# A fused attention and MLP kernel: GELU's steps queued by a clock of GpSimd's queue, output units in pieces of 7, 8 and 9, up pairs in one and in two double steps, and a block's last up pair amid the units in front of it

## The chip, the cores and the metric

The kernel runs on one core of a Trainium2 chip. A core has five engines with a queue each, which take their instructions in program order: TensorE (PE, matrix products; PEld are its weight loads), VectorE (DVE), ScalarE (ACT), GpSimd (POOL) and SyncE (SP, which here only issues DMAs). They meet through semaphores. The metric is the time of one execution in device microseconds (us), as the median of several runs.

## What is computed

The output mixes an attention and an MLP over the same 2048 tokens of width 576:

```python
def _A_ref(x, wqkv, wo):                     # 32 heads of 18
    q, k, v = split(x @ wqkv)
    p = softmax(einsum("bhqd,bhkd->bhqk", q, k) * 18 ** -0.5)
    return einsum("bhqk,bhkd->bhqd", p, v) @ wo

def _B_ref(x, w1, b1, w2, b2):               # 576 -> 4608 -> 576
    y = layernorm(x)
    return gelu(y @ w1 + b1) @ w2 + b2       # the tanh form of GELU

g = sigmoid((x * gate_w).sum(-1))
return g * A + (1 - g) * B
```

All of it is float32. Where a product needs more than TensorE's rounded float32 gives, an operand is split into a high and a low part, and the product is made of three.

## The kernel before

A prologue of some 270 us makes q, k and v, normalizes x, and stores the parts in DRAM. An epilogue of some 75 us divides by the softmax sums, multiplies by `wo` and mixes. Between them lies the main loop, which is what the change is about.

**The loop's steps.** There are 512 steps: 32 units (a pair of heads and half of the queries) of 16 key chunks. Two steps, an even and an odd one, make a double step, in which the program writes, for PE:

- four *rounds* (`next_round`, `s1_round`, L185): two score products for a later unit, whose row maxima DVE takes (L187). The products go to a pool of three PSUM tiles, and a round uses two of them.
- four *score pairs* (`s2`, L226): the scores of this unit, with the maximum subtracted by two extra rows. They go to one PSUM tile `pss` (there is only one), from which ACT takes the exponential (L228). So a score pair can start only when the exponential before it is done.
- one *P·V* (`pv`, L243): sixteen products of the exponentials of the two steps before with v.
- three *fills* (`fill`): pieces of the MLP. Share 0 closes the even step, shares 1 and 2 lie in the odd one.

Before the change both steps have the same form: round, score pair, then P·V (even) or fill 1 (odd), then round, score pair, then fill 0 or fill 2.

**The MLP in the fills.** `mlp` is a generator. The tokens come in four blocks of 512 (`tb`), the 4608 hidden columns in nine groups of four chunks (`g`); that makes 36 groups. A group has two *up pairs* (`h_pair`, L412; 27 double products, `m` = 0 and 1) and four *output units* (`out_pair`, L481; 24 double products, with a drain of PE in the middle). The order is: up pair 0 of group i, the four units of group i-1, up pair 1 of group i. `cuts` says after which products a unit is interrupted, by the share of the fill in which it begins (`piece`). Before, an output unit that begins in fill 0 has three pieces of eight; up pair 1 has four pieces, and up pair 0 (`last`) as many as bring its end to fill 2. Up pair 1 and the next up pair 0 thus take nine fills, three double steps, and a group seven double steps. When the stream is behind its schedule (`late`), up pair 1 has three pieces, and both take two double steps.

**GELU.** When an up pair has ended, DVE and ACT bring its two halves with the bias from PSUM to the tiles `z` (L431, L432; three buffers). Then follow for each half: square (ACT, L452), `plus(GC0)` (two POOL operations), tanh (ACT, L454), and `parts` (four POOL operations, which give `hh` and `hl`, the parts of the hidden activations). `defer(n, fn)` writes a step n *slots* later, a slot being a call of `run_due`, four to a step. Before, these delays are constants: the tanh stands 7 to 9 slots behind the up pair's end whatever POOL has to do in between.

**The weights.** In the first block the raw weights come from DRAM and are split: ACT rounds (L339), POOL subtracts, and both parts are stored for the later blocks, which reload them (`reload`). `bg` holds these splits; one starts when POOL's estimated load (`load`, lowered by 950 per slot) is under a bound.

**The input of the next block.** `load_y` brings the normalized input to the two tiles `Y`. During a block's last up pair it overwrites them chunk by chunk behind the products that read them; the next up pair reads the new chunks.

Of the kernel before, what the change touches and what calls it, by code (L numbers as in the profile page):

```python
# [16 lines left out]
P = 128  # L17
# [7 lines left out]
TB = 512  # L25
# [18 lines left out]
AHEAD = 1  # L44
# [14 lines left out]
def gated_mix_kernel(ctx: ExitStack, tc: tile.TileContext, x, wqkv, wo, w1, b1, w2, b2, gate_w, out):  # L59
# [61 lines left out]

    bg = []
    load = [0.0]

    def run_due():

        slot[0] += 1
        load[0] = max(load[0] - SLOT, 0.0)
# [5 lines left out]
        while k < len(bg):  # L134
            if load[0] < bg[k][2] and slot[0] >= bg[k][0]():
                bg.pop(k)[1]()
                k = 0
            else:
                k += 1

    def pool_op(n, fn, *args, **kw):

        load[0] += n * (1.25 if fn == nc.gpsimd.tensor_scalar else 2.55)
        fn(*args, **kw)  # L144
# [145 lines left out]
    def mlp():  # L290
# [43 lines left out]
        def split(table, key, pool, shape, raw, src, scr, then):  # L334
# [13 lines left out]
            queue = SLOT if raw[0] == 1 else 100 * SLOT  # L348
# [42 lines left out]
        def h_pair(q, last):  # L391
# [16 lines left out]
            ends = cuts(27, (3, 5, 4)[piece[0]] if last else 3 if late and not open_pairs[0] else 4)  # L408
# [17 lines left out]
            open_pairs[0] = 1  # L426

            lag = 0 if m else 2
# [4 lines left out]
            for h in (1, 0):  # L433
                z = zs[h]
                w = zp.tile([P, TB], F32, name="zz", bufs=3)
                hh = hp.tile([P, TB], F32R, name="hh")
                hl = hp.tile([P, TB], F32R, name="hl")
# [7 lines left out]
                def parts(w=w, z=z, hh=hh, hl=hl, h=h, j=2 * m + h):  # L445
# [8 lines left out]
                defer(7 + lag - h, lambda w=w: nc.scalar.activation(w, w, AF.Tanh, scale=GC1))  # L454
                defer(9 + lag - 2 * h, parts)
# [3 lines left out]
        def out_pair(i, t, acc):  # L459
# [5 lines left out]
            ends = cuts(24, (3, 2, 4)[piece[0]])  # L465
# [39 lines left out]
        def outs(i):  # L505
# [4 lines left out]
            for t in range(4):  # L510
                yield from out_pair(i, t, ACC[tb])
# [16 lines left out]
        q = 0  # L528
        for i in range(n + 1):
            for part in range(2):  # L530
                if i < n:
                    tb, g = seq[i]
                    for m in range(AHEAD) if part == 0 else range(AHEAD, G // 2):
                        prep(q + 2)
                        last = i > 0 if part == 0 else m == G // 2 - 1 and i + 1 == n
                        yield from h_pair(q, last)
                        q += 1
                        if g == NG - 1 and m == G // 2 - 1:
# [495 lines left out]
```

## Time and profile before

| | |
|---|---|
| time, median of three runs | 2476.18 us (2474.2 to 2478.33) |
| the profiled execution | 2478.72 us, its span 2476.9 us |
| granted TensorE clock, mean | 0.982 |
| busy: PE, DVE, ACT, POOL | 2367.3, 1665.6, 1363.3, 965.1 us |
| weight loads on PE | 1604.0 us |
| DMA traffic | 330.40 MB, 133 GB/s in the mean |

The span reaches from the first to the last instruction. PE is busy for 96% of it, but its instructions overlap and their ends are modelled, so a busy PE can still be held up: it shows in the distance from the start of one instruction to the start of the next. In rows of a timeline the first number is the start in us from the span's beginning, the second the duration of the merged group, and behind x stands how many instructions are merged; what stands in brackets is idle time of the engine before them, and what ended it.

### The profile page before, as it was taken

The page shows a single profiled execution, that of the slowest core. Times are in us where ns is not written, and L with a number is a line of the kernel's source. Part 1 is how long each engine was busy: PE and PEld are TensorE (multiplying, and loading weights), DVE is VectorE, ACT ScalarE, POOL GpSimd, SP SyncE. Part 2 cuts the span into 40 slices and gives each one's busy share as a digit, 9 for nine tenths or more (in the row PEclk, how much of TensorE's full clock was granted, in tenths as well). Part 3 has the DMA queues.
Part 4 walks back from the last instruction along what each step waited for, and adds up shares of the span by engine and source line. Part 5 has one row for each costly group of instructions (what it writes and reads, how often), then busy time and mean ns, then how long its engine had stood idle before and what let it go on. Part 6 is the DMA issues. An engine that isn't in the chain of part 4 may idle for free.

```text
span 2476.9 us, 50614 instructions
## 1 busy us (share of the span) xinstructions
PE 2367.3 (96%) x20585; PEld 1604.0 (65%) x20585; DVE 1665.6 (67%) x2890; ACT 1363.3 (55%) x1604; POOL 965.1 (39%) x964
## 2 busy tenths in 40 slices
PE   8998999999999999999999999999989999999978
PEld 7876656666665666666666666666656666666538
DVE  4467566667666777776767777777757777777515
ACT  4222466666665566655655665656546556566551
POOL 3001455555553443333444444333343333444310
PEclk9999899999999999999999999999989999999989
DMA  7747645444456423242264333232364332331245
GB/s 231 243 157 222 187 157 149 126 131 138 127 178 175 131 90 112 92 138 97 96 162 144 107 108 111 90 111 96 106 180 126 115 114 101 93 132 46 70 149 200
DMA packets 164506, 330.40 MB, mean 133 GB/s; under 512 B 57826, under 2 KB 84486, under 8 KB 153438
## 3 DMA queue, kind: packets, MB, share of 16 engines
q1 hardware_dynamic: 161970, 322.45, 42.1%
q10 hardware_dynamic: 2304, 4.72, 0.5%
q8 instruction: 162, 2.65, 0.5%
q14 instruction: 70, 0.57, 0.1%
HBM read 234.31 MB, written 96.73 MB: 134 GB/s over the span
## 4 chain that ended last, share of the span: by engine, by line
PE 62%; DMA 4%; issue 3%; ACT 2%; DVE 2%; POOL 1%; SPq 0%; ACTq 0%; POOLq 0%
PE ps L481 15%; PE ps L243 15%; PE ps L412 14%; PE pss L226 9%; PE ps L185 8%; DMA big<-y_scr 2%; PE ps L940 2%; DVE m L187 1%; ACT p L228 1%; ACT z L432 1%; POOL zz L144 1%; ACT ring L228 0%; DMA x<-in_B_w_dram 0%; DMA ka<-ot_scr 0%; POOL w L144 0%
## 5 line engine op out<-in xcount | busy, mean ns | idle before, releaser
L187 DVE TENSOR_REDUCE m<-ps 128x1 f32<-128x512 f32 x2048 | 1315.7, 685 | 548.9 <-PE ps L185 541.8
L228 ACT ACTIVATE p<-pss 128x1024 f32<-128x1024 f32 x684 | 700.2, 1024 | 530.8 <-PE pss L226 530.5
L412 PE MATMUL ps<-big,w 64*128 64x512 f32 x3888 | 539.1, 400 | 23.0 <-ACT z L432 11.5
L481 PE MATMUL ps<-w,hh 64*128 64x288 f32 x4608 | 514.8, 298 | 13.2 <-issue 0.5
L144 POOL TENSOR_SCALAR zz<-zz 128x512 f32<-128x512 f32 x288 | 178.2, 619 | 878.3 <-ACT zz L452 719.8
L226 PE MATMUL pss<-qa,ka 56*128 56x512 f32 x2048 | 466.5, 433 | 42.6 <-ACT p L228 25.9
L185 PE MATMUL ps<-ka,qa 54*128 54x512 f32 x2048 | 478.3, 427 | 13.0 <-DVE m L187 5.6
L228 ACT ACTIVATE ring<-pss 128x1024 f32<-128x1024 f32 x340 | 348.1, 1024 | 257.9 <-PE pss L226 257.8
L412 PEld LDWEIGHTS ps<-big,w 64*128 64x128 f32 x3888 | 400.6, 188 | 109.9 <-ACT z L432 25.2
L481 PEld LDWEIGHTS ps<-w,hh 64*128 64x128 f32 x4608 | 394.4, 185 | 70.0 <-issue 47.2
L144 POOL TENSOR_TENSOR zz<-zz,z 128x512 f32<-128x512 f32 x288 | 370.4, 1286 | 24.0
L185 PEld LDWEIGHTS ps<-ka,qa 54*128 54x128 f32 x2048 | 220.1, 186 | 231.0 <-DVE m L187 195.2
L243 PE MATMUL ps<-p,vt 128*32 128x512 f32 x2736 | 351.0, 608 | 1.4 <-DMA vt<-v_scr 1.4
L481 PE MATMUL ps<-w,hl 64*128 64x288 f32 x2304 | 351.1, 292 | 0.0
L226 PEld LDWEIGHTS pss<-qa,ka 56*128 56x128 f32 x2048 | 209.4, 188 | 147.2 <-ACT p L228 85.2
L144 POOL TENSOR_TENSOR w<-x,w 128x576 fp32r<-128x576 f32 (+1 forms) x54 | 98.4, 1837 | 381.6 <-ACT w L339 207.7
L481 PEld LDWEIGHTS ps<-w,hl 64*128 64x128 f32 x2304 | 227.4, 185 | 5.2
L144 POOL TENSOR_TENSOR hl<-zz,hh 128x512 fp32r<-128x512 f32 x144 | 186.7, 1296 | 12.0
L243 PE MATMUL ps<-ring,vt 128*32 128x512 f32 x1360 | 182.9, 610 | 0.0
L243 PEld LDWEIGHTS ps<-p,vt 128*32 128x32 f32 x2736 | 72.1, 110 | 153.5 <-issue 151.2
L490 DVE SCALAR_TENSOR_TENSOR x<-ps,x 128x288 f32<-128x288 f32 x256 | 105.1, 452 | 23.7 <-PE ps L481 23.1
L702 PE MATMUL ps<-big,wqk 128*128 128x512 f32 x432 | 111.7, 408 | 2.3 <-ACT wqk L623 1.8
(93 smaller groups left out, 1296.7 us busy)
## 6 DMA issues: line engine op xcount, KB each, us to landing
w<-w_scr SPq DMA_DIRECT2D x54, 1152.0 KB
w<-w_scr SPq DMA_DIRECT2D x108, 576.0 KB
x<-in_B_w_dram SPq DMA_DIRECT2D x72, 288.0 KB
w_scr<-w SPq DMA_DIRECT2D x18, 1152.0 KB
w_scr<-w SPq DMA_DIRECT2D x36, 576.0 KB
qa<-qk_scr SPq DMA_DIRECT2D x192, 72.0 KB
ka<-qk_scr SPq DMA_DIRECT2D x90, 144.0 KB
qk_scr<-hh SPq DMA_DIRECT2D x36, 256.0 KB
```

What stands on the lines that cost most here:

```text
L144: fn(*args, **kw)
L185: nc.tensor.matmul(ps, qa[r0:r0 + 54, t * P:(t + 1) * P], ka[r0:r0 + 54, kb * TB:(kb + 1) * TB], start=True, stop=True)
L187: nc.vector.tensor_reduce(M4[u][:, h, t, kb:kb + 1], ps, axis=AX.X, op=ALU.max)
L226: nc.tensor.matmul(ps[:, h, :], ka[r0:r0 + 56, kc * P:(kc + 1) * P], qa[r0:r0 + 56, qb * TB:(qb + 1) * TB], start=True, stop=True)
L228: nc.scalar.activation(RING[n % 3][:, qb], ps, AF.Exp, scale=SCALE)
L243: nc.tensor.matmul(OB[u][r:r + 32, :], v[:, k, 19 * h:19 * h + 32], RING[c % 3][:, qb, h, :], start=(k == 0), stop=(k == NT - 1))
L412: nc.tensor.matmul(ps[h], wt[w_][r, c, :], Y[s_][r, c, :], start=(k == 0), stop=(k == 26))
L432: nc.scalar.activation(zs[0], ps[0], AF.Identity, bias=b[0])
L481: nc.tensor.matmul(ps[nn][:, :ND], h_[r, tok], w_[p_][r, cs[nn]], start=(k == 0), stop=(k == 6 * G - 1))
L490: nc.vector.scalar_tensor_tensor(dst, ps[nn][:, :ND], 0.5, b2b[:, cs[nn]] if g == 0 else dst, op0=ALU.mult, op1=ALU.add)
L702: nc.tensor.matmul(ps, w_[:, c, ms], big[:, s_, :], start=(k == 0), stop=False)
L940: nc.tensor.matmul(ps[:, :ND], OT[b][2][:, s_, tok], w_part(w_, c)[:, cs], start=(k == 0), stop=(k == 13))
```

## The change

It has four parts.

1. **A clock of GpSimd's queue.** `run_due(ns)` advances `now` by an estimate of the PE time since the last call (462, 2080, or the fill's own work, at least 1130), and `pool_op` keeps `pool_end`, when POOL's queue will be done. The tanh is written when `now` has passed the end of its `plus(GC0)` by 200 ns, each half for itself; `parts` two slots behind it; the hidden tile counts as there 1000 ns before POOL's modelled end. A split of W2 starts when POOL's queue is under 3.8 us, one of W1 under 0.95 us (before: 95 and 0.95).
2. **The pieces.** An output unit that begins in fill 0 has pieces of 7, 8 and 9. Up pair 1 has three pieces of nine (one double step), the next up pair 0 six of 4, 5, 5, 4, 5, 4 (two double steps; five if late). One that begins in fill 2 is not cut.
3. **The even step.** Score pair and round change places behind P·V: round, score pair, P·V, score pair, round, fill 0.
4. **A block's last up pair** (`inner`) stands between the second and the third output unit, instead of behind the fourth. Since `hp` has no free tile then, its `hh` and `hl` lie in a W1 tile (`extra`), and W1 is prefetched one pair less ahead in the group behind it (`held`).

The core of the diff:

```diff
-    def run_due():
+    def run_due(ns=SLOT):
         slot[0] += 1
-        load[0] = max(load[0] - SLOT, 0.0)
+        now[0] += ns
+        due = [f for t, f in timed if t <= now[0]]
+        timed[:] = [(t, f) for t, f in timed if t > now[0]]
+        for f in due:
+            f()
...
-            if load[0] < bg[k][2] and slot[0] >= bg[k][0]():
+            if pool_end[0] - now[0] < bg[k][2] and slot[0] >= bg[k][0]():
...
-        load[0] += n * (1.25 if fn == nc.gpsimd.tensor_scalar else 2.55)
+        pool_end[0] = max(pool_end[0], now[0]) + n * (1.36 if fn == nc.gpsimd.tensor_scalar else 2.7)
...
-            queue = SLOT if raw[0] == 1 else 100 * SLOT
+            queue = raw[0] ** 2 * SLOT
...
-            ends = cuts(27, (3, 5, 4)[piece[0]] if last else 3 if late and not open_pairs[0] else 4)
+            ends = cuts(27, (5, 5, 4)[piece[0]] if last else (3, 5, 4)[piece[0]])
+            if last and piece[0] == 0 and not late:
+                ends = {4, 9, 14, 18, 23}
...
-                    defer(4, lambda: HT.update({(i, j): (hh, hl)}))
+                    queue_end(-1000.0, lambda: HT.update({(i, j): (hh, hl)}))
...
+                def first(w=w, z=z, parts=parts):
+                    plus(GC0, w, z)
+                    queue_end(200.0, lambda: second(w, parts))
+                def second(w, parts):
+                    nc.scalar.activation(w, w, AF.Tanh, scale=GC1)
+                    defer(2, parts)
                 defer(2, lambda w=w, z=z: nc.scalar.activation(w, z, AF.Square))
-                defer(4 - h, lambda w=w, z=z: plus(GC0, w, z))
-                defer(7 + lag - h, lambda w=w: nc.scalar.activation(w, w, AF.Tanh, scale=GC1))
-                defer(9 + lag - 2 * h, parts)
+                defer(4 - h, first)
...
-            ends = cuts(24, (3, 2, 4)[piece[0]])
+            ends = {7, 15} if piece[0] == 0 else cuts(24, (3, 2, 1)[piece[0]])
...
+                if t == 2:
+                    yield from between        # the inner up pair
...
             s2(u, kc, 0)
-            run_due()
+            run_due(462.0)
             if kc % 2:
                 fill(step, 1)
             elif step > 0:
                 pv(step - 2)
...
-            run_due()
-            next_round()
+                run_due(2080.0)
+            if kc % 2:
+                next_round()
             s2(u, kc, 1)
-            run_due()
+            if kc % 2 == 0:
+                next_round()
+            run_due(462.0)
             fill(step, 2 if kc % 2 else 0)
```

**An even step on PE**, in a double step with an output unit, in the second block. `ps<-ka,qa` is a round, `pss<-qa,ka` a score pair, `32x512` P·V, `ps<-w,hh` and `ps<-w,hl` the output unit. Before:

```order
L243 MATMUL ps<-p,vt_109 32x512 x4
L243 MATMUL ps<-ring_2331,vt_109 32x512 x4
L185 MATMUL ps<-ka_107,qa_105 128x512 x2
L226 MATMUL pss<-qa_104,ka_107 128x512 x2
L481 MATMUL ps<-w_11009,hh 128x288 x4
L481 MATMUL ps<-w_11009,hl 128x288 x2
L481 MATMUL ps<-w_11011,hh 128x288 x4
L481 MATMUL ps<-w_11011,hl 128x288 x2
L481 MATMUL ps<-w_11015,hh 128x288 x4
L185 MATMUL ps<-ka_107,qa_105 128x512 x2
L226 MATMUL pss<-qa_104,ka_107 128x512 x2
```

The same place with the change:

```order
L253 MATMUL ps<-p,vt_109 32x512 x4
L253 MATMUL ps<-ring_2331,vt_109 32x512 x4
L236 MATMUL pss<-qa_104,ka_107 128x512 x2
L195 MATMUL ps<-ka_107,qa_105 128x512 x2
L505 MATMUL ps<-w_11002,hh 128x288 x4
L505 MATMUL ps<-w_11002,hl 128x288 x2
L505 MATMUL ps<-w_11004,hh 128x288 x4
L505 MATMUL ps<-w_11004,hl 128x288 x2
L505 MATMUL ps<-w_11008,hh 128x288 x2
L195 MATMUL ps<-ka_107,qa_105 128x512 x2
L236 MATMUL pss<-qa_104,ka_107 128x512 x2
```

The score pair now follows P·V at once and the round comes after it; the fill behind them has 14 products (seven pairs) instead of 16, so two rounds stand with only that fill between them.

**ACT's queue around an up pair's end in the first block.** `z<-ps,b1t` takes a half of the up pair from PSUM, `zz<-z` are the squares, `zz<-zz` the tanh, `w<-x` the rounding of raw W2, the rest exponentials. Before:

```order
L432 ACTIVATE z<-ps,b1t 128x512
L228 ACTIVATE p<-pss 128x1024
L452 ACTIVATE zz<-z 128x512 x2
L339 ACTIVATE w_4205<-x 128x576
L339 ACTIVATE w_4208<-x 128x576
L228 ACTIVATE p<-pss 128x1024 x2
L454 ACTIVATE zz<-zz 128x512 x2
L228 ACTIVATE p<-pss 128x1024
```

With the change:

```order
L446 ACTIVATE z<-ps,b1t 128x512
L238 ACTIVATE ring_2331<-pss 128x1024
L478 ACTIVATE zz<-z 128x512 x2
L238 ACTIVATE ring_2331<-pss 128x1024
L238 ACTIVATE p<-pss 128x1024
L349 ACTIVATE w_4219<-x 128x576
L349 ACTIVATE w_4222<-x 128x576
L476 ACTIVATE zz<-zz 128x512
L238 ACTIVATE p<-pss 128x1024
L476 ACTIVATE zz<-zz 128x512
```

The rounding of W2 has moved behind two more exponentials, and so POOL's subtraction, which follows it there, has moved behind `plus(GC0)`; the two tanh no longer stand together.

**SP's queue at the end of the second block.** `w<-w_scr 128x1152` reloads a W2 chunk, `128x2304` a W1 pair, `big<-y_scr` is `load_y`, `dn`, `ot_scr` and `qa` belong to the attention. Before:

```order
L113 DMA w_15496<-w_scr 128x1152
L113 DMA w_15498<-w_scr 128x1152
L113 DMA w_15500<-w_scr 128x1152
L113 DMA w_15502<-w_scr 128x1152
L113 DMA big<-y_scr 64x2x512 x8
L113 DMA big<-y_scr 64x3x512 x4
L257 DMA dn<-oe 128x1x16
L263 DMA ot_scr<-oe 18x512 x4
L113 DMA big<-y_scr 64x2x512 x4
```

With the change:

```order
L113 DMA qa_103<-mr 1x8x128 x4
L113 DMA big<-y_scr 64x3x512 x12
L267 DMA dn<-oe 128x1x16
L273 DMA ot_scr<-oe 18x512 x4
L113 DMA qa_105<-qk_scr 18x1024 x6
L113 DMA w_15691<-w_scr 128x1152
L113 DMA w_15693<-w_scr 128x1152
L113 DMA w_15695<-w_scr 128x1152
L113 DMA w_15697<-w_scr 128x1152
```

The new block's input now stands ahead of the W2 reload instead of behind it, and two output units lie between its last issue and the up pair that reads it.

More of the change, by code (lines that the diff above doesn't have):

```diff
@@ L122, in gated_mix_kernel, with queue_end @@
     bg = []
-    load = [0.0]
-    def run_due():
-        slot[0] += 1
-        load[0] = max(load[0] - SLOT, 0.0)
+    now = [0.0]
+    pool_end = [0.0]
+    timed = []
+    def queue_end(margin, fn):
+        timed.append((pool_end[0] + margin, fn))
+    def run_due(ns=SLOT):
+        slot[0] += 1
+        now[0] += ns
[3 more added lines that the diff above has]
+            f()
         due = [f for s, f in later if s <= slot[0]]
@@ L426, in h_pair @@
             open_pairs[0] = 1
-            lag = 0 if m else 2
+            if inner:
+                extra = wp1.tile([P, 2, 9, P], F32R, name="w4").rearrange("p a b c -> p (a b c)")
             zs = [zp.tile([P, TB], F32, name="z") for _ in range(2)]
@@ L435, in h_pair @@
                 w = zp.tile([P, TB], F32, name="zz", bufs=3)
-                hh = hp.tile([P, TB], F32R, name="hh")
-                hl = hp.tile([P, TB], F32R, name="hl")
+                if inner:
+                    hh, hl = [extra[:, (2 * h + k) * TB:(2 * h + k + 1) * TB] for k in range(2)]
+                else:
+                    hh = hp.tile([P, TB], F32R, name="hh")
+                    hl = hp.tile([P, TB], F32R, name="hl")
                 def plus(c, w, z):
@@ L527, in mlp, with pair @@
         yield 1
-        q = 0
-        for i in range(n + 1):
[L530 to L538, printed above, removed]
-                            hidden[0] = tb
-                if part == 0:
-                    prep(q + 2)
-                    if i > 0:
-                        yield from outs(i - 1)
-                    if 0 < i < n:
-                        prep_w2(i)
+        def pair(q, ahead, last=False, inner=False):
+            prep(q + ahead)
+            yield from h_pair(q, last, inner)
+            i, m, _ = chunk(q)
+            if m == 1 and seq[i][1] == NG - 1:
+                hidden[0] = seq[i][0]
+        for i in range(n + 1):
+            q = 2 * i
+            inside = i < n and seq[i][1] == NG - 1
+            held = 1 if 0 < i < n and seq[i][1] == 0 else 2
+            if i < n:
+                yield from pair(q, held, last=i > 0)
+                prep(q + 1 + held)
+            if i > 0:
+                yield from outs(i - 1, pair(q + 1, 2, inner=True) if inside else ())
+            if 0 < i < n:
+                prep_w2(i)
+            if i < n and not inside:
+                yield from pair(q + 1, held)
     stream = [mlp()]
```

12 lines of the change are left out of this document (7 added, 5 removed).

## Prediction, made before the changed kernel had run

> **What bounds the kernel now.** I read the page first, then busy time by stretches, then timelines of single double steps.
>
> ```profile
> span 2476.9 us, 50614 instructions
> ```
>
> The profiled execution took 2478.72 us, 1.8 over its span and 2.5 over the median of 2476.18. I cut the loop where P·V begins, since there is one per double step. Columns of such rows: length of the stretch, busy time of PE, PEld, DVE, ACT, POOL, granted clock, DMA share, GB/s.
>
> ```profile
> 893.28:909.61 16.33, 15.96 (x132) 10.66 (x130) 11.84 (x20) 11.27 (x14) 9.42 (x10) 1.00 0.35 110
> 884.47:909.61 25.14, 24.77 (x206) 16.44 (x204) 17.31 (x29) 15.37 (x18) 9.42 (x10) 1.00 0.44 150
> 909.61:940.53 30.92, 30.58 (x322) 20.49 (x320) 23.63 (x42) 18.64 (x21) 13.45 (x15) 1.00 0.12 44
> 1109.63:1119.85 10.22, 10.22 (x89) 6.91 (x87) 5.57 (x10) 4.40 (x5) 0.00 (x0) 1.00 0.60 214
> ```
>
> This is one undisturbed group: three double steps for its two up pairs (25.14, the last two of them 16.33), then four with output units (30.92, so 7.73 each), together 56.06. PE is busy for all but 0.7 of it. The fourth row is a double step with an up pair of the pressed form, three pieces of nine products, where PE has no gap at all. So PE's own stream is the bound, and what can be won is where it stands a little, or long.
>
> ```profile
> 271.50:820.20 548.70, 514.01 (x4656) 335.45 (x4656) 370.79 (x629) 337.21 (x397) 302.61 (x277) 0.98 0.49 149
> 820.20:1329.60 509.40, 500.19 (x4697) 332.08 (x4697) 369.81 (x631) 303.39 (x345) 208.51 (x220) 1.00 0.39 119
> ```
>
> The first block (62 double steps) takes 39.3 longer than the second (also 62), with the same products, POOL at 302.6 against 208.5 and PE idle for 35 against 9. That is the second thing to explain.
>
> Inside a steady double step:
>
> ```profile
> 1030.02 1.07 PE L243 MATMUL ps<-ring,vt 128*32 128x512 f32 x8
> ...
> 1031.88 0.50 PE L185 MATMUL ps<-ka,qa 54*128 54x512 f32 x2
> ...
> 1032.21 0.40 PE L226 MATMUL pss<-qa,ka 56*128 56x512 f32 x2
> ...
> 1032.45 0.43 PE L481 MATMUL ps<-w,hh 64*128 64x288 f32 x4
> ...
> 1032.65 1.03 ACT L228 ACTIVATE p<-pss 128x1024 f32<-128x1024 f32 x1 [1.16 <-PE pss L226]
> ...
> 1033.51 0.40 PE L185 MATMUL ps<-ka,qa 54*128 54x512 f32 x2
> 1033.73 0.19 PEld L226 LDWEIGHTS pss<-qa,ka 56*128 56x128 f32 x2 [0.16 <-ACT p L228]
> 1033.74 0.49 PE L226 MATMUL pss<-qa,ka 56*128 56x512 f32 x2
> ...
> 1033.93 1.29 DVE L187 TENSOR_REDUCE m<-ps 128x1 f32<-128x512 f32 x2 [0.24 <-PE ps L185]
> 1034.07 0.30 PE L481 MATMUL ps<-w,hl 64*128 64x288 f32 x2
> ...
> 1034.33 1.02 ACT L228 ACTIVATE ring<-pss 128x1024 f32<-128x1024 f32 x1 [0.65 <-PE pss L226]
> ...
> 1035.47 0.41 PE L185 MATMUL ps<-ka,qa 54*128 54x512 f32 x2
> ...
> 1035.71 0.41 PE L226 MATMUL pss<-qa,ka 56*128 56x512 f32 x2
> ...
> 1035.94 0.31 PE L481 MATMUL ps<-w,hh 64*128 64x288 f32 x2
> ...
> 1037.00 0.41 PE L185 MATMUL ps<-ka,qa 54*128 54x512 f32 x2
> ...
> 1037.31 0.51 PE L226 MATMUL pss<-qa,ka 56*128 56x512 f32 x2
> ...
> 1037.74 1.04 PE L243 MATMUL ps<-p,vt 128*32 128x512 f32 x5
> ```
>
> The starts give 1.86 for P·V, then round 0.33, score pair 0.24, fill 1.06, round 0.23, score pair 0.33, fill 1.40 (PE drains within it), round 0.24, score pair 0.23, fill 1.06, round 0.31, score pair 0.43: 7.72. A round or score pair takes 0.23 to 0.24, and 0.33 beside a P·V, on either side. Above that are 0.10 in the second score pair (its weights wait for ACT), 0.08 in the last round and 0.10 in the last score pair: 0.28 in which PE waits for the exponential before. That cycle, from one exponential's start to the next, is 1.68 here; at another such place it is 1.62:
>
> ```profile
> 1025.02 1.03 ACT L228 ACTIVATE ring<-pss 128x1024 f32<-128x1024 f32 x1 [0.32 <-PE pss L226]
> ...
> 1026.64 1.03 ACT L228 ACTIVATE p<-pss 128x1024 f32<-128x1024 f32 x1 [0.60 <-PE pss L226]
> ```
>
> I take 1.65: two score pairs closer than that make PE wait.
>
> **The change, part by part.** No product is added or removed; the double steps stay 256, and nearly all have one of the forms above: by the order of the two programs 141 output steps (140 before), and 33 up triplets (32 before). The few odd ones I put at the same time before and after.
>
> *Swap and pieces of 7, 8, 9.* An output product pair is 1.06/8 = 0.1325, so the fills become 0.93, 1.40 and 1.19. The step is 1.86 + 0.33 (score pair) + 0.24 (round) + 0.93 + 0.23 + 0.23 + 1.40 + 0.24 + 0.23 + 1.19 + 0.23 + 0.33 = 7.44. The distances of score pairs are now 1.63 over the short fill (0.23 + 0.24 + 0.93 + 0.23, since the round stands there too), 1.86 and 1.65, and over P·V 2.2: the exponential just fits everywhere.
>
> But two rounds now stand only 0.24 + 0.93 = 1.17 apart, with three PSUM tiles for four products. By the rows above DVE starts 0.42 behind a round (1033.51, 1033.93) and frees the first tile after half of 1.29, at 1.07. What a round does that meets such a wait:
>
> ```profile
> 1132.22 1.29 DVE L187 TENSOR_REDUCE m<-ps 128x1 f32<-128x512 f32 x2 [1.23 <-PE ps L185]
> ...
> 1132.97 0.18 PEld L185 LDWEIGHTS ps<-ka,qa 54*128 54x128 f32 x1 [0.51 <-DVE m L187]
> ```
>
> The weights start when the first maximum is done (1132.22 + 0.65, and a hand-over of some 0.1), and their 0.18 is exposed. So the second product's weights start at about 1.17, just when it was due. The delay lies between 0 and 0.18 + 0.1 = 0.28. I take 0.10, the difference of the round at 1031.88 (0.50 long) from that at 1033.51 (0.40), since the due time and the release all but meet. The output step becomes 7.54, 0.19 less: 141 x 0.19 = 27.
>
> [...]
>
> *Up pairs.*
>
> ```profile
> 2314.30 2.26 PE L412 MATMUL ps<-big,w 64*128 64x512 f32 x18
> 2316.40 0.40 PE L185 MATMUL ps<-ka,qa 54*128 54x512 f32 x2
> ```
>
> Nine product pairs take 2.10, one 0.233. The single double step is the 10.22 above. With 14 pairs (4, 5, 5) a step is 10.22 - 13 x 0.233 = 7.19, with 13 (4, 5, 4) 6.96. The score pairs around a fill of five are 0.23 + 1.17 + 0.23 = 1.63 apart, 0.02 short; around the closing fill of four 1.39, 0.26 short; the DVE wait is 0.10 in each. That gives 7.33 and 7.34, the triplet 24.89 against 25.14: 33 x 0.25 = 8.
>
> Every up pair now ends in fill 2. Its z, and the two squares two slots later, come to ACT between the exponentials around P·V: three operations of about 0.63 (the length of the tanh rows below), 1.9, into the 2.3 of that distance less an exponential, 1.03, so 1.27, plus about 0.4 in which the z runs ahead. The second exponential is 0.25 late, of which 0.1 is slack: 0.15 x 72 pairs = 11 lost. Ends for it are 0 and 0.25. Steady term: 27 + 8 - 11 = 24, ends -14 (delays of 0.28 in all short steps) and 58 (none of the three).
>
> *GELU by POOL's clock.* In the first block:
>
> ```profile
> 410.75 2.80 POOL L144 TENSOR_TENSOR w<-x,w 128x576 fp32r<-128x576 f32 x2 [9.02 <-ACT w L339]
> ...
> 415.65 0.63 ACT L454 ACTIVATE zz<-zz 128x512 f32<-128x512 f32 x1 [1.89 <-POOL zz L144]
> ...
> 417.71 0.63 ACT L454 ACTIVATE zz<-zz 128x512 f32<-128x512 f32 x1 [1.42 <-POOL zz L144]
> ...
> 419.30 0.50 PE L226 MATMUL pss<-qa,ka 56*128 56x512 f32 x2 [2.45 <-ACT p L228]
> ```
> ```profile
> 412.63:424.55 11.92, 9.47 (x67) 5.89 (x65) 4.69 (x9) 5.53 (x7) 11.08 (x13) 0.86 0.80 142
> 419.30:422.70 3.40, 3.40 (x20) 2.67 (x22) 0.69 (x2) 1.28 (x2) 3.15 (x5) 0.62 0.64 126
> ```
>
> POOL subtracts two W2 chunks (2.80) ahead of the first GELU steps; the two tanh stand at a fixed slot, wait 1.89 and 1.42 for POOL in ACT's queue, the exponential behind them waits too, and with it a score pair, 2.45. Then PE runs at a granted clock of 0.62 for 3.4. The double step takes 11.92; the two of its kind in the quiet group take 16.33, 8.2 each, so a stall costs 3.7.
>
> [...]
>
> Now the tanh is written when `now` has passed POOL's end, and `now` advances 462 + 462 + 2080 + 462 + 462 and the fills, 7.4 in an output step against 7.54 worked out: it runs a little behind PE, which is the safe side. What goes is bounded by 0 and 33 (39.3 less the 10.4 and plus the 4.5 of the input waits below). The roundings of W1 and W2 stay on ACT, two of W2 and a tanh now in one gap between exponentials (1.9 into some 0.65): about 1.3, and as much again for the others, so 2 of the 3.7 a group. I take 16 of 33. If POOL falls behind, `z` (three buffers) is late next.
>
> *The last up pair amid the units.*
>
> ```profile
> 768.47:795.17 26.70, 21.03 (x133) 11.66 (x131) 11.49 (x18) 12.90 (x16) 14.11 (x14) 0.88 1.05 283
> 1285.60:1306.43 20.83, 18.11 (x133) 10.66 (x131) 11.85 (x20) 11.35 (x14) 11.35 (x12) 1.00 0.97 227
> 1799.22:1829.58 30.36, 22.99 (x131) 12.74 (x130) 11.95 (x19) 11.52 (x14) 11.31 (x12) 0.84 1.02 253
> ```
> ```profile
> 1797.25 17.27 SPq L113 DMA_DIRECT2D big<-y_scr  x16
> ```
>
> These are the two double steps around the change of the input. They should take 16.33, so they lose 10.4, 4.5 and 14.0: 28.9. PE waits for y while the DMA share is about 1. At 253 GB/s, 30.36 us are 7.7 MB, the input and the four W2 chunks issued ahead of it; 17.27 for SP to issue 16 loads is itself a bound. With the change 12 loads, 13 us by the same rate, begin a third into the pair, and two output steps (15.1) follow before the first new product. Two thirds of the pair's 10.2 and that make 22, and the products go through the chunks in 14 more. The W2 reload then comes later, and has the 14.7 of one up pair where it had 25; it is a third of those 7.7 MB, 10 us. I leave 4 of 28.9 for it and for the qa loads behind it, and take 25; ends 5 and 29. The W1 prefetch, one pair less ahead in a block's first group, is hidden by the four output steps in front of the pair that needs it (30 us), `extra` is written by POOL alone, and the new bound on W2 splits in the first block moves them behind GELU's steps on POOL, where an up pair still lies ahead of their use: nothing for these. POOL issues no DMA here.
>
> Sum: 24 + 16 + 25 = 65, so 2413.7 for the profiled execution, 2411 against the median.
>
> **The rivals.**
> - *The rounds' weights hide* (and the squares): no DVE delay, 207 short steps x 0.10 = 21 more, 2390. For it: release and due time nearly meet; against: the row at 1132.97. [...]
> - *The swap gives nothing*: DVE delay of 0.22 instead of 0.10 eats the 24, 2435. For it: the maxima of a round take 1.29, and those rounds are 1.17 apart. Against: the 2.2 over P·V let DVE catch up.
> - *Stalls stay or move*: tanh still late, since POOL's clock doesn't see that a subtraction waits for a raw load: 2411 + 16 = 2427; or W2's reload is late at each block's start: up to 2436.
> - *Slower*: GELU is too slow for up pairs 14.7 apart in place of 16. The second pair's z needs a buffer that POOL's last product of the first pair frees; if DVE waits for it, the maxima and so the rounds wait. Over 65/36 = 1.8 lost in each group decides; 2.3 give 2411 + 83 = 2494. For it: POOL is busy for 11.08 of 11.92 in that window. Against: it is at 41% in the second block, so it would have to lose twice that in the first alone.
>
> **How the numbers follow.** The forecast (2398 to 2423) has 0.53, weights hidden (2375 to 2398) 0.17, swap without gain 0.12, stalls that stay or move 0.10 (both 2423 to 2440), slower 0.05, none of it 0.03. The time is that of the likeliest, 2411. A range of 2378 to 2438 leaves out the slow tail and a corner at the low end. Faster by over 0.2% (5 us, about what a measurement here can tell from no change) is 0.92, the same 0.03, slower 0.05.
>
> **What would show it.** Output steps of 7.5 from P·V to P·V; rounds behind the short fill with products of 0.50; the up triplet at 24.9; tanh rows without POOL as releaser and no clock under 1 in the first block, which then takes some 520; the steps after a change of input near 15, with no wait for y. I am wrong if output steps stay at 7.7, if ACT waits for POOL as before, if the first output unit of a block waits for W2, or if DVE's z waits for POOL.

## The result, and the profile after

The changed kernel takes 2412.14 us (median of four runs, 2409.13 to 2416.81), the kernel before 2475.19 beside it: a ratio of 0.9742, 95% interval 0.9729 to 0.9755. The forecast was 2411. The profiled execution took 2409.13, its span is 69.7 shorter than that of before. (It is the shortest of the four; between the medians the difference is 63.)

```profile
span 2407.2 us, 50590 instructions
```

**The steady loop.** Busy time by stretches (columns as before): four output steps, then the three double steps of two up pairs.

```profile
1042.35:1072.74 30.39, 30.07 (x322) 21.43 (x320) 23.73 (x43) 18.58 (x21) 11.39 (x12) 1.00 0.45 114
1072.74:1097.64 24.90, 24.89 (x206) 16.43 (x204) 16.79 (x31) 15.40 (x18) 11.40 (x12) 1.00 0.39 136
```

30.39 stands against 30.92, so an output step takes 7.60 where it took 7.73 here. The up triplet takes 24.90 against 25.14, and PE now has no gap in it. The same output step in the timeline:

```profile
1049.96 1.06 PE L253 MATMUL ps<-p,vt 128*32 128x512 f32 x8
...
1051.81 0.50 PE L236 MATMUL pss<-qa,ka 56*128 56x512 f32 x2
...
1052.15 0.40 PE L195 MATMUL ps<-ka,qa 54*128 54x512 f32 x2
...
1052.36 1.03 ACT L238 ACTIVATE p<-pss 128x1024 f32<-128x1024 f32 x1 [1.27 <-PE pss L236]
1052.39 0.43 PE L505 MATMUL ps<-w,hh 64*128 64x288 f32 x4
...
1052.58 2.48 DVE L197 TENSOR_REDUCE m<-ps 128x1 f32<-128x512 f32 x4
...
1053.19 0.32 PEld L195 LDWEIGHTS ps<-ka,qa 54*128 54x128 f32 x2
1053.32 0.51 PE L195 MATMUL ps<-ka,qa 54*128 54x512 f32 x2
...
1053.55 0.51 PE L236 MATMUL pss<-qa,ka 56*128 56x512 f32 x2
...
1053.79 0.41 PE L505 MATMUL ps<-w,hh 64*128 64x288 f32 x2
...
1054.32 0.40 PE L505 MATMUL ps<-w,hl 64*128 64x288 f32 x2
1054.80 0.30 PEld L505 LDWEIGHTS ps<-w,hh 64*128 64x128 f32 x4 [0.31 <-issue]
...
1055.30 0.41 PE L195 MATMUL ps<-ka,qa 54*128 54x512 f32 x2
...
1057.18 0.45 PE L236 MATMUL pss<-qa,ka 56*128 56x512 f32 x2
```

Score pair and round have changed places at 1051.81, and the fill between the rounds is the 0.93 that was forecast. DVE takes four maxima in one go from 1052.58; the first is done at about 1053.20, where the weights of the second round stand (0.32 for two, instead of 0.19), and its products are 0.51 long instead of 0.40. From there everything on PE is 0.10 later, which comes to light at the drain: fill 1 lasts from 1053.79 to the round at 1055.30, 1.51, where it was 1.40.

**Where the 69.7 went.** Times by starts of P·V, the 256 double steps numbered from 0:

| double steps | before | after | difference |
|---|---|---|---|
| 0 to 5 (start) | 54.2 | 59.3 | +5.1 |
| 6 to 51 (first block) | 402.5 | 372.9 | -29.6 |
| 52 to 61 (first change of input) | 92.0 | 86.0 | -6.0 |
| 62 to 114 | 432.9 | 421.9 | -11.0 |
| 115 to 123 (second change) | 76.4 | 70.8 | -5.6 |
| 124 to 177 | 436.9 | 430.0 | -6.9 |
| 178 to 189 (third change) | 113.4 | 100.6 | -12.8 |
| 190 to 241 | 424.2 | 415.4 | -8.8 |
| 242 to 254 (end) | 107.2 | 117.0 | +9.8 |

The remaining 3.9 lie around the loop. Two stretches are longer than before, and the forecast had priced neither.

**The end.** The last four units now follow the four before them at once, and their W2 is asked for only there:

```profile
2254.05 2.72 SPq L113 DMA_DIRECT2D qa<-mr  x4
...
2256.87 1.81 SPq L113 DMA_DIRECT2D w<-w_scr  x4
...
2260.86 0.85 PE L505 MATMUL ps<-w,hh 64*128 64x288 f32 x4 [6.72 <-DMA w<-w_scr]
```

PE stands for 6.72 and then for two shorter waits at half its pace (0.85 for four products instead of 0.43, at a granted clock of 0.50 from 2260.86 to 2269.00): that double step, in which no rounds are left, takes 18.99, where the three behind it take 7.32 to 7.40.

**The start.** A rounding of W1 stands in ACT's queue ahead of an exponential. The view names no releaser for its wait ("issue"), but SP issues its raw load only at 285.80, and by the trace the packets of that load (512 bytes each) run from 291.53 to 294.47, so the load hasn't landed before:

```profile
295.39 1.16 ACT L349 ACTIVATE w<-x 128x1152 fp32r<-128x1152 f32 x1 [6.19 <-issue]
...
297.52 0.80 PE L236 MATMUL pss<-qa,ka 56*128 56x512 f32 x2 [5.73 <-ACT p L238]
```

**The first block and the changes of input.** The first two rows are the first 62 double steps and the next 62, the other three an output step and the two up steps behind it at each change of input, 22.33 by the middle values.

```profile
269.25:787.50 518.25, 499.69 (x4645) 337.58 (x4645) 366.49 (x630) 337.60 (x397) 302.64 (x277) 0.99 0.51 155
787.50:1280.20 492.70, 489.67 (x4649) 337.47 (x4649) 364.03 (x629) 303.68 (x345) 205.88 (x218) 1.00 0.39 122
...
735.16:764.15 28.99, 24.57 (x201) 15.06 (x199) 17.16 (x31) 14.85 (x17) 10.75 (x11) 0.94 0.59 158
1242.61:1265.00 22.39, 22.29 (x200) 14.83 (x199) 17.52 (x31) 12.79 (x13) 5.98 (x7) 1.00 0.85 230
1743.35:1769.99 26.64, 24.56 (x201) 15.07 (x199) 17.54 (x31) 12.79 (x13) 5.87 (x7) 0.94 0.63 181
```

The three changes lose 6.7, 0.1 and 4.3, together 11 where they lost 28.9. (These are the losses of one execution each: in the traces of the seven kernels of this document that are alike around the third change, double steps 178 to 189 take 97.3 to 103.6.) No product waits for y any more. What PE waits for are small loads that lie behind y's 4.6 MB:

```profile
745.56 0.25 DVE L276 RECIPROCAL dn<-dn 128x16 f32<-128x16 f32 x1 [5.29 <-DMA dn<-oe]
...
746.42 0.65 PE L195 MATMUL ps<-ka,qa 54*128 54x512 f32 x1 [3.85 <-DVE m L197]
...
1752.75 0.87 PE L236 MATMUL pss<-qa,ka 56*128 56x512 f32 x2 [1.99 <-DMA qa<-mr]
```

At 745 DVE stands at a reciprocal for an 8 KB load, the maxima stand behind it, and PE behind these; at 1752 it is the rows of the maxima for the next unit.

### The profile page after: what moved, and what is told of

The parts are those of the page before. It is cut to its first block, busy times and chain, and to the rows that moved or that the text cites. A ratio compares the mean times of both kernels' runs of the same rounds, so it can differ in the third digit from the quotient of the medians.

```text
span 2407.2 us, 50590 instructions
## 1 busy us (share of the span) xinstructions
PE 2326.7 (97%) x20585; PEld 1622.1 (67%) x20585; DVE 1647.6 (68%) x2890; ACT 1364.4 (57%) x1604; POOL 964.8 (40%) x964
## 4 chain that ended last, share of the span: by engine, by line
PE 88%; DMA 4%; DVE 4%; ACT 2%; issue 1%; SPq 1%; ACTq 0%; DVEq 0%
PE ps L505 20%; PE ps L253 19%; PE ps L425 17%; PE pss L236 12%; PE ps L195 11%; PE ps L732 4%; PE ps L753 2%; PE ps L970 1%; DVE m L197 1%; ACT p L238 1%; DMA big<-y_scr 1%; PE ps L659 1%; ACT w L349 1%; DMA dn<-oe 1%; SPq L113 0%
## 5 line engine op out<-in xcount | busy, mean ns | idle before, releaser
L197 DVE TENSOR_REDUCE m<-ps 128x1 f32<-128x512 f32 x2048 | 1296.8, 683 | 460.4 <-PE ps L195 458.0
L425 PE MATMUL ps<-big,w 64*128 64x512 f32 x3888 | 517.8, 393 | 0.1
L505 PE MATMUL ps<-w,hh 64*128 64x288 f32 x4352 | 499.0, 300 | 19.1 <-DMA w<-w_scr 7.0
L236 PE MATMUL pss<-qa,ka 56*128 56x512 f32 x2048 | 482.7, 438 | 28.3 <-ACT p L238 18.6
L195 PE MATMUL ps<-ka,qa 54*128 54x512 f32 x2048 | 461.3, 411 | 14.3 <-DVE m L197 8.1
L505 PEld LDWEIGHTS ps<-w,hh 64*128 64x128 f32 x4352 | 400.0, 186 | 76.4 <-issue 51.9
L425 PEld LDWEIGHTS ps<-big,w 64*128 64x128 f32 x3888 | 392.6, 186 | 66.3 <-DVE z L445 0.4
L236 PEld LDWEIGHTS pss<-qa,ka 56*128 56x128 f32 x2048 | 198.6, 186 | 284.0 <-ACT p L238 130.0
L195 PEld LDWEIGHTS ps<-ka,qa 54*128 54x128 f32 x2048 | 240.2, 186 | 49.2 <-DVE m L197 22.1
L505 PEld LDWEIGHTS ps<-w,hl 64*128 64x128 f32 x2176 | 235.1, 185 | 0.2
L154 POOL TENSOR_TENSOR hl<-zz,hh 128x512 fp32r<-128x512 f32 x136 | 176.7, 1300 | 11.4
```

The lines of the kernel that those rows point to most:

```text
L195: nc.tensor.matmul(ps, qa[r0:r0 + 54, t * P:(t + 1) * P], ka[r0:r0 + 54, kb * TB:(kb + 1) * TB], start=True, stop=True)
L197: nc.vector.tensor_reduce(M4[u][:, h, t, kb:kb + 1], ps, axis=AX.X, op=ALU.max)
L236: nc.tensor.matmul(ps[:, h, :], ka[r0:r0 + 56, kc * P:(kc + 1) * P], qa[r0:r0 + 56, qb * TB:(qb + 1) * TB], start=True, stop=True)
L425: nc.tensor.matmul(ps[h], wt[w_][r, c, :], Y[s_][r, c, :], start=(k == 0), stop=(k == 26))
L505: nc.tensor.matmul(ps[nn][:, :ND], h_[r, tok], w_[p_][r, cs[nn]], start=(k == 0), stop=(k == 6 * G - 1))
```

## The experiments

A table of middle values first (medians over the double steps that have the same products in their three fills; the three up steps of a group in their order), since the readings below go by it:

| kernel | output step | up steps |
|---|---|---|
| before | 7.77 (8/8/8) | 8.81, 8.71, 7.71 |
| changed | 7.60 (7/8/9) | 10.22, 7.34, 7.39 |
| fixed slots | 7.60 | 10.22, 8.06, 7.39 |
| old up cuts | 7.60 | 8.82, 8.69, 7.70 |
| no swap | 7.76 | 10.22, 7.43, 7.51 |
| swap, 8/8/8 | 7.62 | 10.21, 7.37, 7.39 |
| no swap, 8/8/8 | 7.77 | 10.21, 7.50, 7.51 |

**The swap without the pieces, the pieces without the swap, neither.** In the first two one of these edits is made, in the third both:

```diff
-            if kc % 2:
-                next_round()
+            next_round()
             s2(u, kc, 1)
-            if kc % 2 == 0:
-                next_round()
```
```diff
-            ends = {7, 15} if piece[0] == 0 else cuts(24, (3, 2, 1)[piece[0]])
+            ends = cuts(24, (3, 2, 4)[piece[0]])
```

> The changed kernel, pieces of 7, 8 and 9, but the round stands ahead of the score pair in every half step again. Theory: an exponential takes 1.65 from start to start, and without the round between them the score pairs around the piece of seven are 0.23 + 0.93 + 0.23 = 1.39 apart, 0.26 short; the 0.10 that the round loses to VectorE is gone. Output steps 7.59 + 0.16 = 7.75, and 66 up steps with a piece of four as much: (141 + 66) x 0.16 = 33, so 2445. Rival: the swap is worth nothing, what is saved for the exponential is lost to VectorE: 2412.

> The changed kernel with the swap, but output units in pieces of 8, 8 and 8. Theory: rounds around the first piece are then 1.30 apart and don't wait for VectorE (products of 0.40 there instead of 0.50), but the score pairs around the last piece are 0.23 + 1.06 + 0.23 = 1.52 apart, 0.13 short: 7.44 + 0.13 = 7.57 against 7.59 measured, 2409 to 2414. So the swap is the gain and the pieces matter little. Rival: it is the pieces that bring the gain, and steps go back to 7.77: 2412 + 141 x 0.17 = 2436.

> The changed kernel with neither the swap nor the pieces of 7, 8 and 9. Theory: output steps are those of before, 7.77, 0.17 more, and the up steps with a piece of four lose 0.16 as without the swap: 141 x 0.17 + 66 x 0.16 = 35, 2447. Rival: the steady step owes its gain to something else in the change (POOL's clock, the squares in other gaps), and little comes back: 2412 to 2425.

Without the swap: 2449.43, ratio to before 0.9879 (0.9863 to 0.9896). With the swap and pieces of eight: 2412.14, 0.973 (0.971 to 0.9749). With neither: 2438.01, 0.9832 (0.9816 to 0.9849). Timeline rows of the first (the second score pair of an output step), then of the second (rounds around the first piece, and the last score pair):

```profile
1060.87 0.19 PEld L236 LDWEIGHTS pss<-qa,ka 56*128 56x128 f32 x2 [0.29 <-ACT p L238]
```
```profile
1054.86 0.40 PE L195 MATMUL ps<-ka,qa 54*128 54x512 f32 x2
...
1056.16 0.40 PE L195 MATMUL ps<-ka,qa 54*128 54x512 f32 x2
...
1059.85 0.19 PEld L236 LDWEIGHTS pss<-qa,ka 56*128 56x128 f32 x2 [0.22 <-ACT p L238]
```

Without the swap the weights of the score pair wait 0.29 for the exponential (0.26 was worked out) and the step is back at 7.76. With pieces of eight the rounds are 1.30 apart, their products are 0.40 and fill 1 is 1.42 again: the 0.10 is the wait for DVE, and it is gone; but the last score pair waits for ACT. So the swap is worth 0.15 to 0.16 a step, and the pieces are worth 0.01 to 0.02: what the short piece gives to the exponential it takes from DVE. In the up steps the swap is worth 0.09 and 0.12 (7.34 and 7.39 against 7.43 and 7.51), where 0.16 was expected. (The step is a cleaner reading than the total: with pieces of eight the last block holds other forms, units of 6/6/6 among them, and the end comes out differently. Of the 11.9 by which the third kernel's span is shorter than the first's, 10.0 lie in double steps 242 to 254, where products wait 3.6 for W2's reload instead of 9.2. In the second kernel these steps take 109.1 instead of 117.0, so that its total equals the changed kernel's although its steps are a little longer.)

So the rival of 2390, in which the rounds' weights hide, doesn't hold for a load that waits for DVE's release here: 0.10 are lost (products of 0.51 at 1053.32 in the changed kernel), and regained when the rounds stand further apart (0.40 at 1056.16 with pieces of eight).

**The old cuts of the up pairs.**

```diff
-            ends = cuts(27, (5, 5, 4)[piece[0]] if last else (3, 5, 4)[piece[0]])
-            if last and piece[0] == 0 and not late:
-                ends = {4, 9, 14, 18, 23}
+            ends = cuts(27, (3, 5, 4)[piece[0]] if last else 3 if late and not open_pairs[0] else 4)
```

> The changed kernel with the old cuts of the up pairs (three of seven products each, then 6, 6, 5 and 6, 5, 5, in place of three of nine and then 4, 5, 5 and 4, 5, 4). Theory: the new cuts are worth what the middle values of the two traces say, 25.23 less 24.95 for three double steps, and the two squares after the pair hide in the gap over P times V: 33 x 0.28 = 9 more, 2421. Rival, the prediction's sum: the cuts bring 8 and the squares cost 11, so the old cuts give 2409. A difference between the old cuts now and the old cuts before is possible, since the swap moves the round in these steps too; then the up triplet's middle value says it.

2441.07, ratio 0.9857 (0.9842 to 0.9871): 29 more than the changed kernel, where 9 were expected. The triplet is 25.21 against 24.95, 0.26 x 33 = 9, as the theory had it, and in the three blocks without splits it is the whole difference: double steps 62 to 114 take 424.0 against 421.9. Of the rest most is in the first block (392.8 against 372.9 for double steps 6 to 51). One output step takes 18.29 there and the step behind it 1.3 too much, because a rounding of W1 waits 10.2 for its raw load, the mechanism of the start at another place. And in each of the seven groups the second and the third up step lose 0.6 and the output step behind them 0.5, 1.7 in all, where the changed kernel loses 0.9. There the tanh waits for POOL again, although it is written by POOL's clock (the last row gives sum, number and longest of ACT's waits):

```profile
408.15 2.81 POOL L154 TENSOR_TENSOR w<-x,w 128x576 fp32r<-128x576 f32 x2 [9.24 <-ACT w L349]
...
413.06 0.63 ACT L473 ACTIVATE zz<-zz 128x512 f32<-128x512 f32 x1 [1.88 <-POOL zz L154]
```
```profile
ACT zz L473 <- POOL zz L154: 11.7, 7, 1.9
```

POOL's clock counts the subtraction of W2 from the time at which it is written, but the subtraction starts only when ACT has rounded, and GELU's steps stand behind it. So the clock alone doesn't keep the tanh from waiting; with the new cuts the subtraction falls behind `plus(GC0)`, and the wait is gone. The first two changes of input take 9.0 longer than in the changed kernel, the start and the end 4.2 less; these weren't taken apart. So the cuts are worth 9 by themselves, and most of the 20 beyond them hangs on where the roundings fell. The squares cost nothing: in the changed kernel (timeline, around P·V behind an up pair)

```profile
1083.25 1.02 ACT L238 ACTIVATE ring<-pss 128x1024 f32<-128x1024 f32 x1
1084.15 1.15 ACT L478 ACTIVATE zz<-z 128x512 f32<-128x512 f32 x2
...
1084.81 0.50 PE L236 MATMUL pss<-qa,ka 56*128 56x512 f32 x2
...
1085.36 1.03 ACT L238 ACTIVATE ring<-pss 128x1024 f32<-128x1024 f32 x1
```

the two take 1.15, not 1.26, the z ran in the gap before, and the exponential begins 0.55 behind its score pair, as long as it takes elsewhere.

**GELU at fixed slots, and the splits without the new bound.**

```diff
-                    queue_end(200.0, lambda: second(w, parts))
...
+                lag = 0 if m else 2
+                defer(7 + lag - h, lambda w=w, parts=parts: second(w, parts))
+                defer(9 + lag - 2 * h, parts)
```
```diff
-            queue = raw[0] ** 2 * SLOT
+            queue = SLOT if raw[0] == 1 else 100 * SLOT
```

> The changed kernel, but GELU's steps stand at fixed slots again (tanh 7 and 9 slots, the last products 9 and 11 slots behind the pair); the new bound on the splits of W2 stays. Theory: POOL's clock is what took the stalls out of the first block. They come back in its groups, tanh with POOL as releaser, about 3 us for each of seven: 2412 + 21 = 2433. Rival: the bound on the splits does it, since it keeps two subtractions of W2 (2.80) from standing in front of GELU's steps: 2412 to 2415, no POOL releaser on tanh.

> The changed kernel, but the splits of W2 go to POOL whatever it has queued, as before the change; GELU's steps stay queued by POOL's clock. Theory: the clock alone is enough, since a tanh is then written later if a subtraction stands in front of it: 2409 to 2415. Rival: the bound does it: tanh waits or up pairs wait for GELU, about 3 us for each of seven groups, 2433.

Fixed slots: 2428.68, ratio 0.9805 (0.9791 to 0.982). Without the bound: 2411.9, 0.9746 (0.9726 to 0.9765), so the bound does nothing that can be seen. The fixed slots (the tanh 6 to 9 slots behind the pair's end, as before) cost 16.5 where 21 was expected, but not where it was expected. Waits of ACT, first in the kernel before, then with fixed slots (columns: sum, times, longest); in the changed kernel no such row is left:

```profile
ACT zz L454 <- POOL zz L144: 27.2, 19, 1.9
```
```profile
ACT zz L475 <- POOL zz L154: 10.8, 27, 1.4
```

With fixed slots the second up step takes 8.06 instead of 7.34 in the three blocks without splits, 0.72 x 26 = 19, and the first block loses 5.4 (378.3 against 372.9 for double steps 6 to 51), 24 together; 8.7 come back at the start, where the rounding of W1 happened to fall right (50.6 against 59.3). The timeline at such a place in the second block:

```profile
1089.72 1.03 ACT L238 ACTIVATE p<-pss 128x1024 f32<-128x1024 f32 x1 [0.72 <-PE pss L236]
...
1090.64 0.62 ACT L475 ACTIVATE zz<-zz 128x512 f32<-128x512 f32 x1
...
1091.59 0.63 ACT L475 ACTIVATE zz<-zz 128x512 f32<-128x512 f32 x1 [0.32 <-POOL zz L154]
1092.12 1.01 ACT L238 ACTIVATE p<-pss 128x1024 f32<-128x1024 f32 x1
...
1093.18 0.50 PE L236 MATMUL pss<-qa,ka 56*128 56x512 f32 x2 [0.45 <-ACT p L238]
```

Both tanh stand between the same two exponentials, and one waits for POOL. By the clock each lies in a gap of its own. The long stalls of the first block come back in full in neither kernel: with fixed slots TensorE's gap in a group is 2.07 once and 1.16 six times, where it is some 0.65 in the changed kernel and was 1.5 to 2.5 before. The old cuts of the up pairs above bring the tanh's wait back in all seven groups with clock and bound in place, at 1.7 a group where the kernel before lost 3.2 to 5.0. So the shape of the steps has a share in what took the stalls away; how the rest divides among the clock, the bound and the swap stays open, since no run undoes them together.

**The last pair of every block outside, and of the last block alone.**

```diff
-            inside = i < n and seq[i][1] == NG - 1
-            held = 1 if 0 < i < n and seq[i][1] == 0 else 2
+            inside = False
+            held = 2
```
```diff
-            inside = i < n and seq[i][1] == NG - 1
+            inside = i + 1 < n and seq[i][1] == NG - 1
```

> The changed kernel, but a block's last up pair stands behind all four output units again, as before the change. Theory: the pair's place pays at the input changes and costs at the end. In the changed kernel's trace the steps around the three changes lose some 11 us where they lost 28.9, and one output step at 2251 stands 11 for a W2 reload that has no up pair in front of it. Undone, the first comes back (+18), the second goes (-8, since the last steps before the change lost about 3 there): 2412 + 10 = 2422. Rival 1: the place is worth the 25 that the prediction gave it, and the stand at 2251 has another cause and stays: 2437. Rival 2: the transfers are as late in either place, only the stand goes: 2404.

> The changed kernel, but the last block's last up pair stands behind its units again; the two in front of a change of input stay amid theirs. Theory: the stand of 11 at 2251 is the reload of W2 for the last four units, which begins when the four before them end and has no up pair in front of it. In the kernel with all pairs outside the last block was 8.0 shorter (524.4 against 532.4 from the same double step on): 2412 - 8 = 2404. Rival: the reload waits for SP's queue, which stands in front of a row of maxima, and an up pair in between changes nothing: 2410 to 2414.

All outside: 2432.57, ratio 0.9821 (0.9806 to 0.9836), between the theory (2422) and its rival (2437). The last block alone: 2406.71, 0.9716 (0.9703 to 0.9729). The two up steps at each change in the first of them, 14.73 by the middle values:

```profile
743.80:771.85 28.05, 20.61 (x120) 10.84 (x118) 11.21 (x18) 12.24 (x16) 14.14 (x14) 0.76 1.04 282
1258.00:1291.25 33.25, 24.13 (x120) 12.64 (x118) 11.25 (x19) 10.96 (x14) 11.32 (x12) 0.69 0.92 222
1777.20:1800.70 23.50, 19.22 (x124) 10.19 (x124) 11.96 (x20) 11.04 (x14) 11.30 (x12) 0.85 0.98 238
```

The weight loads' wait for y in the second of these stretches (sum, times, longest):

```profile
PEld ps L425 <- DMA big<-y_scr: 13.0, 8, 4.2
```

The three stretches lose 13.3, 18.5 and 8.8, 40.6 in all, more than the 28.9 before the change; a likely reason, which no run shows by itself, is that the new cuts bring the next pair sooner. So amid the units the pair is worth 30 in this kernel, and costs 7 at the end. In the second kernel double steps 242 to 254 take 109.8 instead of 117.0, and no product waits for W2 there any more: the stand was the missing up pair in front of the reload.

**Roundings apart, later, and the reciprocal later.** In the first, bookkeeping left out, a rounding goes only into a slot without other late steps, and one into a slot:

```diff
+                if looped[0] and acts:
+                    break
+                acts = 1
                 bg.pop(k)[1]()
```
```diff
-            LOADED[1, q] = slot[0] + (LAND if looped[0] else 5)
+            LOADED[1, q] = slot[0] + (LAND + (4 if q < 4 else 0) if looped[0] else 5)
```
```diff
-        defer(12 if u < NU - 2 else 4, spread)
+        defer(20 if u < NU - 2 else 4, spread)
```

> The changed kernel, but a rounding of W1 or W2 is written only in a slot in which no tanh was, and one in a slot. Theory: the 0.88 that the second step of each up triplet still loses in the first block (8.22 against 7.34, seven times) is two roundings and a tanh in one gap between exponentials, 1.25 and 0.62 into some 0.65: apart they cost a third or less, 2412 - 4 = 2408. Rival: the gaps are full in any case, and 0.62 more in another gap makes another exponential late: 2411 to 2416.

> The changed kernel, but the first four chunks of W1 are rounded four slots (one double step) later behind their loads. Theory: the 16.08 of the third double step (8.65 in the kernel with fixed slots) is a rounding on ACT that waits 6.2 for a raw load, behind which an exponential and 5.7 of TensorE wait; later, the load has landed: 2412 - 6 = 2406. Rival: the load is late by more than that, since SP issues it behind 9.1 of stores, or the up pair then waits for its weights: 2411 to 2418.

> The changed kernel, but a unit's reciprocal on VectorE stands 20 slots behind its load in place of 12. Theory: at the first change of input (the step of 12.26 at 735) the 8 KB load of the denominators lands behind y's 4.6 MB, VectorE stands 5.3 at the reciprocal, and the maxima behind it hold up the round; two double steps later the load is there: 2412 - 4 = 2408. Rival: the load of qa's rows and of the next qa are as late, and take the place of the wait: 2411 to 2414.

Apart: 2410.18, 0.973 (0.9711 to 0.9748). Later by four slots: 2413.98, 0.9738 (0.9725 to 0.9752). Reciprocal: 2408.6, 0.9719 (0.9705 to 0.9732).

With the roundings apart the 0.88 that the second up step still lost in the first block is gone (7.32 in all blocks) and the start takes 49.5 instead of 59.3. But one W1 rounding, at double step 48, now meets its load too early (line numbers are 4 higher here):

```profile
661.98 7.65 SPq L332 DMA_DIRECT2D x<-in_B_w_dram  x2
...
673.83 1.16 ACT L353 ACTIVATE w<-x 128x1152 fp32r<-128x1152 f32 x1 [9.51 <-DMA x<-in_B_w_dram]
...
675.96 0.79 PE L240 MATMUL pss<-qa,ka 56*128 56x512 f32 x2 [9.45 <-ACT p L242]
```

SP issues that load behind the loads for attention, and the exponential behind the rounding waits with it: 10.0 there and 1.1 in the next step. Three double steps that also hold transposes (13, 21 and 45) lose 3.5 more, and together this eats the gain. Four slots more alone were too few: the third double step went from 16.08 to 13.08, not to 8.65, and the total didn't move by what can be told apart. The later reciprocal took the first change of input from 86.0 to 81.2 (double steps 52 to 61), as expected; at the third change nothing moved, since another load is late there.

**Four edits together.** The end, the reciprocal and the roundings apart as above, and 16 slots for W1:

```diff
-            LOADED[1, q] = slot[0] + (LAND if looped[0] else 5)
+            LOADED[1, q] = slot[0] + (2 * LAND if looped[0] else 5)
```

> The changed kernel with four edits: the last block's last up pair behind its units, the reciprocal at 20 slots, a rounding only in slots without a tanh and one in a slot, and W1's roundings 16 slots behind their loads in place of 8. Theory: with the roundings apart alone, the start came back by 9.8 (double steps 0 to 6 took 49.5 against 59.3) and the 0.88 of the up triplets went, 6 in all, but one rounding of W1 then met a load that landed late behind the loads for attention, 10.3 and 1.1 after it; 16 slots take that away. With 7.2 at the end (109.8 against 117.0) and 4.8 at the first change of input (81.2 against 86.0): 2412 - 10 - 6 - 7 - 5 = 2384, and 2387 if the places mix as they did in the runs of the single edits. Rival: a rounding of W1 waits for its load again at another place, or a pair then waits for its weights, 10 each: 2394 to 2400.

2387.35 (2381.88 to 2389.33), ratio to before 0.9638 (0.9625 to 0.9651): faster than both kernels. Its start takes 49.4, double steps 6 to 51 370.9, the first change 79.4, the end 109.9, and no rounding waits long (1.1 at most in the loop). The second up step takes 7.58 to 7.72 there in six groups of the first block and 8.83 in its first group, against 7.32 with the roundings apart alone, so not all of the 0.88 is gone.

## Why the prediction was right, point by point

The sum was 65, the span moved by 69.7 (63 between the medians). The swap and the place of the pair carry about what they were said to carry, and runs that undo them show it; for GELU's clock the runs show less. The terms are less good than their sum:

- *Swap and pieces*: 27 forecast, 141 x 0.17 = 24 by the middle values. The wait for DVE was taken as 0.10 and is 0.10, for the reason given. The step came at 7.60 instead of 7.54; 0.05 of that is the last score pair (0.38 to the next P·V instead of 0.33). That the pieces matter was wrong: the step was worked out for both together, and the swap alone gives nearly all of it.
- *Up pairs*: 8 forecast, 0.28 x 33 = 9.
- *Squares*: 11 lost by the forecast, nothing found. The failed step is the sum of 1.9 into 1.27; the z doesn't belong into that gap, and two squares in a row take 1.15.
- *GELU*: 16 of 33. What double steps 8 to 53 take over the middle values of their forms fell from 31 to 8, so 23. The 2 us a group left for roundings and tanh in one gap were the right mechanism at half the size, 0.88. The price of a stall was taken too low: 11.92 was set against 8.2, the mean of two unlike up steps, and against its own form (7.71) it is 4.2. And the clock isn't shown to be what took the stalls away: with the old cuts the tanh waits for POOL in spite of it, by the third rival's mechanism, with a rounding on ACT in place of a raw load. What the clock is shown to be worth is 0.72 in every group without splits, since it puts the two tanh of a pair into two gaps. The forecast didn't see that the old slots would not fit the new step.
- *Changes of input*: 25 of 28.9 forecast, 18 found. No product waits for y, as said, but 11 are lost to small loads behind y's, where 4 had been left.
- *W2's reload*: the forecast gave it the time of one up pair. At the program's end it has none; this is the "reload late" of the third rival, at one place instead of three, and cost 7 to 10.
- *The start*: a rounding on ACT that waits for its raw load cost 5 against before. No term had it.

So 33 instead of 24, 23 instead of 16 and 18 instead of 25, less 15 for two waits that were overlooked, makes 59 of the 66 that the loop lost; the other 7 lie in the odd forms (double steps with transposes, at the units' seams) and aren't taken apart. That the total came out within 0.1% is in part luck: errors of 7 to 15 had both signs. (The ends given for the steady term, -14 and 58, come out of its own figures as some -13 and 56; nothing hangs on that.)

Of the signs that were named, output steps of 7.5 came as 7.60, the round's 0.50 as 0.51, the triplet as 24.90, the first block as 518.25, no POOL releaser on tanh; the steps after a change near 15 came at the second change alone (14.79). The clock of the first block was to stay at 1 and is 0.99 (it is 0.50 in the 3 us behind the wait of 5.73 at the start, and 0.53 in those behind that of 3.85 at the first change). Of the signs of being wrong, an output unit that waits for W2 came, at the last units of the program instead of a block's first.

## What to carry to other kernels

Where two engines take turns on one resource (here one score tile, which TensorE writes and ACT reads), look at the time between its uses, and put something else between two uses that stand too close: that the round stands behind the score pair instead of in front of it was worth 0.16 in 7.77, without an instruction less. A step that is moved next to a queue which the bound engine needs (ACT's exponentials, DVE's maxima) must not wait for a transfer there: at three places of these kernels a rounding or a reciprocal, small itself, stood at a fixed distance behind a load and held up 4 to 10 us of TensorE. A model of an engine's queue that adds up its own work alone, as POOL's clock does, misses the time for which that work waits for another engine. When the order changes, look at the first and the last round of the loop by themselves, since what covers a load in the middle may not be there.

## What was not expected of the hardware

It was not expected behind how short a stand of TensorE the granted clock would be low, nor that it would not be low behind every stand of that length: the forecast priced the stalls of the first block by the one at 419.30. A gap of PE in each of the seven groups of that block, in both kernels, and two gaps of the changed kernel at the changes of input, with the granted clock of the 3 us from the end of the gap:

| kernel | end of the gap | gap | granted clock behind it |
|---|---|---|---|
| before | 352.50 | 1.53 | 1.00 |
| before | 419.30 | 2.45 | 0.64 |
| before | 480.58 | 2.37 | 0.67 |
| before | 541.79 | 2.43 | 0.71 |
| before | 602.75 | 2.03 | 1.00 |
| before | 662.24 | 2.42 | 0.54 |
| before | 724.54 | 2.43 | 1.00 |
| changed | seven, from 354.24 to 693.65 | 0.64 to 0.66 | 1.00 each |
| changed | 746.42 | 3.85 | 0.53 |
| changed | 1752.75 | 1.99 | 0.63 |

So the length of a gap alone doesn't tell the clock behind it here: behind 2.43 it was 0.71 at one place and 1.00 at another, and behind 1.99 it was 0.63 where behind 2.03 it was 1.00. These rows don't show what decides. At the second change of input with the pair outside the loss was more than the wait: TensorE's weight loads waited 13.0 for y, and the two steps lost 18.5, at a mean granted clock of 0.69.
